# Tying staged weight loads to the first attention's last copy to x

## The chip, the cores and the metric

One NeuronCore of a Trainium2 chip runs the whole program. The metric is device time in microseconds (us) of one execution. Medians are over single runs; all runs of this case were of the fast state. Where two kernels are compared, the ratio is the mean time of one kernel's fast runs over that of the other's of the same rounds, so it is not quite the ratio of the medians quoted beside it. Its 95% interval follows in brackets.

## The reference, cut to what matters

```python
# attention: (batch, heads, seq, dim) = (4, 8, 768, 48), a gated linear recurrence
f = 1.0 / (1.0 + np.exp(-f_logit))
for t in range(S):
    state = f[:, :, t, :, None] * state + np.einsum('bhd,bhe->bhde', k[:, :, t], v[:, :, t])
    y[:, :, t] = np.einsum('bhd,bhde->bhe', q[:, :, t], state)
x = y.transpose(0, 2, 1, 3).reshape(B, S, H * D)          # (4, 768, 384)
# mixer, per batch
u  = x + (x.transpose(0, 2, 1) @ U @ V).transpose(0, 2, 1)
ch = np.maximum(u @ w_ch1, 0.0) @ w_ch2                   # 384 -> 1536 -> 384
return u + ch
```

The weights arrive as 64-bit floating-point numbers and are turned into 32-bit ones on the chip. The attention inputs are 32-bit already.

## The kernel before

Four batches, each of four pairs of heads (16 "units"). The attention of batch 0 runs first, alone; its mixer runs while the attention of batch 1 goes on, and so forth. The change touches the seam between the attention of batch 0 and its mixer. There, weights come in by loads of 384 KB, called pieces here: w1 pieces 0 to 11, of 128 columns each. `start` issues a load; `end` converts it, with two instructions on ACT (lines L90, L91), three on DVE and one on GpSimd.

```python
def start():                                  # weight_loader
    raw = pool.tile([P, WP], U64, name="w_raw", bufs=RAW) if place is None else place()
    raw = T["raw"] = raw[0:rows, 0:n]
    dma.dma_start(out=shaped(raw), in_=w)
def end():
    ...
    nc.scalar.activation(f, hi.bitcast(F32), AF.Abs)                 # L90
    nc.scalar.activation(r, lo, AF.Copy, scale=2.0**-29)             # L91
    nc.vector.tensor_scalar(...)              # three on DVE
    nc.gpsimd.tensor_tensor(...)
# ahead_by(n, loads): call i starts load i + n and ends load i
```

The first six w1 pieces are staged in the "zw" buffers, which nobody needs yet, two pieces to a buffer; all others share four "w_raw" buffers.

```python
FIRST = 6                                     # early = 3: U and two parts of V
weights += [take_in(w1[:, :, i * P : (i + 1) * P], w1_rows[...], place if i < FIRST else None) for i in range(NFC)]
...
for n in range(HP):                           # the attention of batch 0, units 0 to 3
    ...
    if n == 1:
        for start, _ in weights[: early + 2]: # U, V, V, w1 pieces 0 and 1
            start()
    elif n > 1:
        load(n + 2, "f", "k", "q", "v")       # inputs of units 4 and 5
for start, _ in weights[early + 2 : early + FIRST]:   # w1 pieces 2 to 5
    start()
loads = ahead_by(early + FIRST, weights)
for piece in rear(HP - 1, "read") + loads[:2] + rear(HP - 1, "inner") + loads[2 : early + 1]:
    piece()                                   # "inner" of unit 3 ends with the last copy to x
loads = loads[early + 1 :]
m = mixer(0)
start = m.before[:5] + m.firsts[0:1] + m.before[5:]
idles = {1: 1, 2: 1}
for i, (_, piece) in enumerate(start + m.firsts[1:]):
    busy(idles.get(i, 0))                     # idle matmuls
    piece()
    if loads and i != 1:
        loads.pop(0)()                        # one conversion (and one more start) a step
    ...
```

The steps of `start` are: 0 the low-rank product (ph), 1 its sum (ph), 2 the mixing (pu, and the additions to x on DVE), 3 and 4 two turns of x (put on TensorE, copy uT on ACT), 5 the first product with w1 (pz), 6 the third turn. In the traces TensorE, DVE and ACT run these steps in the order of the program (ACT in the kernel before: h at 52.05 us, piece 2 at 52.76 and 53.22, uT at 55.55). The order in which SyncE issues transfers is fixed when the program is built, from the program's order and a model of what is ready when; the trace of the kernel before has it so, from q of unit 5 at 47.08 over pieces 2 and 3 at 47.96, v at 50.73 and pieces 4 and 5 at 52.82 to pieces 6 and 7 from 54.46 on.

Of the kernel before, what the change touches and what calls it, by code (L numbers as in the profile page):

```python
# [10 lines left out]
F32 = mybir.dt.float32  # L11
U32 = mybir.dt.uint32
U64 = mybir.dt.uint64
# [5 lines left out]
WP = 384  # L19
# [82 lines left out]
def ahead_by(n, loads):  # L102


    def call(i):
        if i + n < len(loads):
            loads[i + n][0]()
        loads[i][1]()

    return [lambda i=i: call(i) for i in range(len(loads))]  # L110
# [322 lines left out]
def factored_path(ctx, tc, q, k, v, f_logit, moe_U, moe_V, moe_w_ch1, moe_w_ch2, out, ok):  # L433
# [4 lines left out]
    nc = tc.nc  # L438
    B, H, S, D = q.shape
    P = nc.NUM_PARTITIONS  # L440
# [4 lines left out]
    HP = H // 2  # L445
# [4 lines left out]
    NFC = FF // P  # L450
# [17 lines left out]
    zp = ctx.enter_context(tc.tile_pool(name="zp", bufs=3))  # L468
# [21 lines left out]
    def load(n, *names):  # L490

        b, hp = divmod(n, HP)
        for nm in names:
            if nm == "v":
                v_tiles[n] = three.tile([P, NBL, 2, D], F32, name="v_nat")
            for par in range(2):
                head = src[nm][b, 2 * hp + par]
                if nm == "v" and par:

                    for s in range(2):  # L500
                        nc.sync.dma_start(
                            out=v_tiles[n][(1 - s) * C : (2 - s) * C, :, par, :],
                            in_=head.rearrange("(c s p) d -> s p c d", s=2, p=C)[s],
                        )
                    continue
                if nm == "v" or n < TURNED:
                    dst = v_tiles[n] if nm == "v" else nat[n % 2][nm]
                    nc.sync.dma_start(out=dst[:, :, par, 0:D], in_=head.rearrange("(c p) d -> p c d", p=P))
                    continue
                head = head.rearrange("(c i) d -> i c d", i=NB)  # L510
                for part in range(2):
                    p0 = par * PAD + part * NB
                    n_ch = min(NB, D - part * NB)
                    nc.sync.dma_start(
                        out=raw[n % 2][nm][p0 : p0 + NB, :].rearrange("p (c d) -> p c d", d=NB)[:, :, 0:n_ch],
                        in_=head[:, :, part * NB : part * NB + n_ch],
                    )
# [43 lines left out]
    table = one.tile([P, 1], F32, name="table")  # L561
# [7 lines left out]
    weights = [take_in(U, moe_U.rearrange("(c p) r -> p c r", p=P))]  # L569
    weights += [take_in(*pair) for pair in by_rows(V, moe_V, R)]  # L570
    early = len(weights)
    w1_rows = moe_w_ch1.rearrange("(c p) f -> p c f", p=P)

    spare = []

    def place():
        if not spare:
            t = zp.tile([P, NFC // 2, 2 * P], F32, name="zw").rearrange("p i t -> p (i t)").bitcast(U64)
            spare.extend([t[:, 0:WP], t[:, WP : 2 * WP]])
        return spare.pop(0)  # L580

    FIRST = 6
    weights += [
        take_in(w1[:, :, i * P : (i + 1) * P], w1_rows[:, :, i * P : (i + 1) * P], place if i < FIRST else None)
        for i in range(NFC)
# [96 lines left out]
    def mixer(b):  # L682
        return Mixer(tc, b, x_tiles[b], U, V, w1, w2, sums if b else None, ident, blocks, out, two, three, zp, ps_big, ps_mm,
                     b == 0, z_all, room if b >= B - 2 else None, FEWER - (b - B + 2) * NCH // 4)
# [172 lines left out]
    def front(n, *names):  # L857

        if n >= NU:
            return []  # L860
        if n not in ahead:
            ahead[n] = dict(zip(("gates", "keep", "keys", "read_back", "queries"), prepare(n)))
        return [ahead[n].pop(nm) for nm in names]

    def rear(n, *names):

        if not 0 <= n < NU:
            return []
        if n not in here:
            here[n] = dict(zip(("kept", "states", "scan", "scores", "read", "inner"), attend(n)))  # L870
        return [here[n].pop(nm) for nm in names if nm in here[n]]

    def steps(first, last):


        for n in range(first, last):
            yield from rear(n - 1, "scores") + rear(n, "kept") + front(n + 1, "gates", "keep", "keys")
            yield from rear(n - 1, "read")
            made = rear(n, "states", "scan")
            yield lambda: [f() for f in made]  # L880
            yield from front(n + 1, "read_back", "queries") + rear(n - 1, "inner")
            if n + 2 < NU:
                load(n + 2, "v")

    def attention(pieces, portions, todo):

        fill = Fill(todo, portions)
        for piece in pieces:
            fill()
            piece()  # L890
        fill.rest()
# [10 lines left out]
    def start_mixer(b, after):  # L902

        m = mixer(b)
        n = len(after) // 4
        pieces = after[:n] + m.before[:1] + after[n : 2 * n] + m.before[1:2] + after[2 * n : 3 * n]
        pieces += m.before[2:3] + after[3 * n :] + m.before[3:]
        for _, piece in pieces:
            piece()
        return m  # L910
# [4 lines left out]
    with tc.manual_schedule(engines={nc.vector.engine, nc.scalar.engine}):  # L915


        idle = ps_mm.tile([P, 512], F32, name="idle", tag="mm")

        def busy(n):  # L920
            for _ in range(n):
                nc.tensor.matmul(idle[:, 0:DM], lhsT=ident, rhs=ends[:, 0:DM], start=True, stop=True)  # L922

        busy(1)
        for piece in front(0, "gates"):
            piece()
        for n in range(HP):
            pieces = front(n, "keep", "keys") + rear(n - 1, "scan", "scores")
            pieces += [lambda: busy(3)] + rear(n, "kept") + front(n, "read_back", "queries")
            if n + 1 < HP:  # L930
                pieces += front(n + 1, "gates") + rear(n - 1, "read", "inner") + rear(n, "states")
            else:
                pieces += rear(n, "states") + rear(n - 1, "read") + rear(n, "scan", "scores") + rear(n - 1, "inner")
            for piece in pieces:
                piece()
            if n < 2:
                load(n + 2, "v")
            if n == 1:


                for start, _ in weights[: early + 2]:
                    start()
            elif n > 1:
                load(n + 2, "f", "k", "q", "v")
        for start, _ in weights[early + 2 : early + FIRST]:
            start()
        loads = ahead_by(early + FIRST, weights)
        for piece in rear(HP - 1, "read") + loads[:2] + rear(HP - 1, "inner") + loads[2 : early + 1]:
            piece()
        loads = loads[early + 1 :]  # L950

# [4 lines that stand above are left out]
        EARLY = 9  # L956
        second = chain(front(HP, "gates", "keep", "keys", "read_back", "queries"), steps(HP, 2 * HP + 1))
        for i, (_, piece) in enumerate(start + m.firsts[1:]):
            busy(idles.get(i, 0))
            piece()  # L960
            if loads and i != 1:
                loads.pop(0)()
            if i >= EARLY:
                next(second)()
        for f in loads:
            f()
        n = len(m.seconds) // (NBL // 2)
        todo, after = m.seconds[:-n], m.seconds[-n:]

        attention(second, 12 + 10 * HP - (len(start) + len(m.firsts) - 1 - EARLY), todo)  # L970
        m = start_mixer(1, after)
        for f in to_sum:
            f()
# [325 lines left out]
@with_exitstack  # L1299
def kernel(  # L1300
    ctx: ExitStack,
    tc: tile.TileContext,
    q: bass.AP,
    k: bass.AP,
    v: bass.AP,
    f_logit: bass.AP,
    moe_U: bass.AP,
    moe_V: bass.AP,
    moe_w_ch1: bass.AP,
    moe_w_ch2: bass.AP,  # L1310
    out: bass.AP,
):


    nc = tc.nc
    args = (q, k, v, f_logit, moe_U, moe_V, moe_w_ch1, moe_w_ch2, out)
    flag = ctx.enter_context(tc.tile_pool(name="flag", bufs=1))
    ok = flag.tile([1, 1], I32, name="ok")
    with ExitStack() as inner:
        factored_path(inner, tc, *args, ok)  # L1320
    good = nc.values_load(ok[0:1, 0:1], min_val=0, max_val=1)
    with tc.If(good == 0):
        with ExitStack() as inner:
            general_path(inner, tc, *args)
# [30 lines left out]
```

## Time and profile before

| | before |
|---|---|
| median of the first three runs (range) | 492.71 us (492.5 to 496.79) |
| span of the profiled run | 490.9 us |
| TensorE (PE) busy | 472.4 us, 96% |
| DVE, ACT, GpSimd busy | 73%, 33%, 7% |

The head of the profile's page of the kernel before (busy us, share of the span, instructions):

```profile
span 490.9 us, 12677 instructions
...
PE 472.4 (96%) x5519; PEld 402.0 (82%) x5519; DVE 356.1 (73%) x561; ACT 163.4 (33%) x307; POOL 36.3 (7%) x49
```

TensorE's timeline at the seam (start, duration, engine, line, operation, out<-in, how many instructions; in brackets the idle time before and what ended it):

```profile
52.67 1.56 PE L197 MATMUL pu<-h,V 32*128 32x384 f32 x12
54.64 1.74 PE L207 MATMUL put<-ident,x 128*128 128x128 f32 x12 [0.40 <-DVE x L187]
56.49 2.83 PE L219 MATMUL pz<-uT,w 128*128 128x256 f32 x12
59.16 0.82 PE L207 MATMUL put<-ident,x 128*128 128x128 f32 x6
```

PE is the engine to look at, the others have room. It goes from pu over the turns into pz with one gap of 0.40 us. From there on it is full (busy for all of the 55.5 us from 56.5 to 112), so the seam is where time can be won or lost. The four lines of the timeline are the ones to compare later.

### The profile page before, as it was taken

To read this page: it belongs to the slowest core of one execution; us is meant where nothing else is said; L and a number is where in the kernel's file an instruction comes from. 1 tells how busy PE (TensorE), PEld (TensorE's weight loads), DVE (VectorE), ACT (ScalarE), POOL (GpSimd) and SP (SyncE) were. 2 spreads that over 40 slices of the span, in tenths; PEclk is the share of its full clock that TensorE was granted. 3 is DMA by queue.
4 is the path that set the end of the run, shared out by engine and by line. 5 is a ranking of instruction groups with operands and counts; after the bars stand their busy time and mean duration, and the time that the engine had idled before them with its cause. 6 is when DMAs were issued, how large, how long until landed. Compare 5 with 4: busy or idle time off the path is not lost.

```text
span 490.9 us, 12677 instructions
## 1 busy us (share of the span) xinstructions
PE 472.4 (96%) x5519; PEld 402.0 (82%) x5519; DVE 356.1 (73%) x561; ACT 163.4 (33%) x307; POOL 36.3 (7%) x49
## 2 busy tenths in 40 slices
PE   7997999999999999999999999999989999999995
PEld 4775688886666568898898788889969999999995
DVE  5886789788998667656855449796876796948642
ACT  3434675564443223423242322442311212112200
POOL 3001345451000000000000000000000000000000
PEclk9999999999999999999999999999989999999998
DMA  9989976685768422424534100100000000000001
GB/s 144 158 172 172 260 183 147 158 153 65 113 106 123 83 41 37 62 27 91 65 49 81 25 33 1 27 3 19 18 2 0 34 2 16 17 1 33 0 34 38
DMA packets 158679, 34.34 MB, mean 70 GB/s; under 512 B 149206, under 2 KB 157078, under 8 KB 158614
## 3 DMA queue, kind: packets, MB, share of 16 engines
q1 hardware_dynamic: 158614, 33.44, 37.3%
q8 instruction: 45, 0.74, 0.7%
q14 instruction: 20, 0.16, 0.1%
HBM read 28.70 MB, written 4.72 MB: 68 GB/s over the span
## 4 chain that ended last, share of the span: by engine, by line
PE 90%; DVE 4%; DMA 2%; issue 1%; ACT 1%; SPq 0%; DVEq 0%; ACTq 0%
PE pw L273 25%; PE pz L219 23%; PE pp L371 12%; PE po L244 10%; PE y L823 3%; PE y L841 3%; PE ds L785 3%; PE sc L748 3%; PE pt L620 2%; PE idle L922 2%; PE put L207 2%; PE pt L769 2%; DMA late<-in_f_logit_dram 1%; PE pu L197 1%; DMA late<-in_k_dram 1%
## 5 line engine op out<-in xcount | busy, mean ns | idle before, releaser
L219 PE MATMUL pz<-uT,w 128*128 128x256 f32 x504 | 115.8, 384 | 0.1
L219 PEld LDWEIGHTS pz<-uT,w 128*128 128x128 f32 x504 | 93.4, 190 | 13.2 <-issue 0.3
L273 PE MATMUL pw<-zw,w_raw 128*128 128x192 f32 x216 | 37.4, 328 | 0.8 <-DVE o L187 0.8
L273 PE MATMUL pw<-w,z_all 128*128 128x192 f32 x216 | 37.8, 330 | 0.2 <-DVE o L187 0.2
L273 PEld LDWEIGHTS pw<-zw,w_raw 128*128 128x128 f32 x216 | 35.2, 190 | 1.6 <-DVE o L187 1.5
L273 PEld LDWEIGHTS pw<-w,z_all 128*128 128x128 f32 x216 | 34.9, 190 | 1.2 <-DVE o L187 0.8
L654 DVE TENSOR_TENSOR_SCAN late<-fz,late 128x768 f32<-128x768 f32 x16 | 28.1, 1755 | 9.7 <-ACT fz L649 5.1
L95 POOL TENSOR_TENSOR w<-w_y,w_r 128x384 int32<-128x384 int32 x24 | 30.2, 1257 | 36.2 <-DVE w_y L94 32.1
L229 ACT ACTIVATE z_all<-pz 128x512 f32<-128x512 f32 x33 | 19.6, 595 | 39.6 <-PE pz L219 39.5
L371 PE MATMUL pp<-v_nat,late 128*128 128x128 f32 x224 | 28.8, 275 | 0.0
L672 DVE TENSOR_TENSOR_SCAN late<-fz,other 128x768 f32<-128x768 f32 x16 | 27.9, 1745 | 0.1
L371 PEld LDWEIGHTS pp<-v_nat,late 128*128 128x128 f32 x224 | 27.0, 192 | 0.0
L244 PE MATMUL po<-w,zw 128*128 128x384 f32 x72 | 25.6, 499 | 0.0
L244 PE MATMUL po<-w,z_all 128*128 128x384 f32 x72 | 25.3, 496 | 0.0
L364 ACT ACTIVATE other<-other 128x512 f32<-128x512 f32 x18 | 11.3, 631 | 40.0 <-DVE other L187 40.0
L811 ACT COPY st<-added 128x576 f32<-128x576 f32 x12 | 14.7, 1226 | 26.0 <-DVE added L806 26.0
L755 DVE TENSOR_TENSOR A<-sc,causal 128x768 f32<-128x768 f32 x16 | 15.2, 947 | 10.5 <-PE sc L748 10.5
L244 PEld LDWEIGHTS po<-w,zw 128*128 128x128 f32 x72 | 12.9, 190 | 8.7 <-issue 1.2
L244 PEld LDWEIGHTS po<-w,z_all 128*128 128x128 f32 x72 | 13.1, 190 | 8.5 <-DVE o L187 0.6
L92 DVE TENSOR_SCALAR w_y<-w_y 128x384 f32<-128x384 f32 (+3 forms) x27 | 11.9, 439 | 10.9 <-ACT w_y L90 10.7
L187 DVE TENSOR_TENSOR w_raw<-z_all 128x768 f32<-128x768 f32 x12 | 11.4, 954 | 10.6 <-ACT z_all L229 9.2
L187 DVE TENSOR_TENSOR w_y<-w_y,pw 128x192 f32<-128x192 f32 x18 | 6.3, 349 | 17.5 <-PE pw L273 17.5
(185 smaller groups left out, 844.7 us busy)
## 6 DMA issues: line engine op xcount, KB each, us to landing
w_raw<-in_moe_w_ch_dram SPq DMA_DIRECT2D x18, 384.0 KB, 4.3
out_dram<-o SPq DMA_DIRECT2D x24, 192.0 KB, 1.9
v_nat<-in_v_dram SPq DMA_DIRECT2D x16, 144.0 KB, 2.8
v_nat<-in_v_dram SPq DMA_DIRECT2D x32, 72.0 KB, 3.0
zw<-in_moe_w_ch_dram SPq DMA_DIRECT2D x6, 384.0 KB, 5.5
late<-in_f_logit_dram SPq DMA_DIRECT2D x10, 96.0 KB, 3.4
late<-in_k_dram SPq DMA_DIRECT2D x10, 96.0 KB, 2.8
late<-in_q_dram SPq DMA_DIRECT2D x10, 96.0 KB, 2.9
```

The source lines that it names most:

```text
L95: nc.gpsimd.tensor_tensor(dst.bitcast(I32), shaped(y.bitcast(I32)), shaped(r), ALU.add)
L187: nc.vector.tensor_tensor(*args)
L219: nc.tensor.matmul(pm[:, i * 2 * P : (i + 1) * 2 * P], lhsT=w1[:, m, o : o + P], rhs=uT[a][:, m, :], start=(m == 0), stop=(m == NDC - 1))
L229: nc.scalar.activation(z[a, c][:, k : k + 2, :].rearrange("p i t -> p (i t)"), pm, AF.Relu)
L244: nc.tensor.matmul(pm, lhsT=z[a, i // NI][:, i % NI, s * P : (s + 1) * P], rhs=w2[:, i, :], start=(i == 0), stop=(i == NFC - 1))
L273: nc.tensor.matmul(pm[:, n * HM : (n + 1) * HM], lhsT=lhs[:, i, :], rhs=rhs[:, i, :], start=(i == 0), stop=(i == NI - 1))
L371: nc.tensor.matmul(pm[:, i, r * P : (r + 1) * P], lhsT=room["w"](wn)[:, r * P : (r + 1) * P], rhs=x_node(a, xn), start=((xn, wn) == of[0]) ...
L654: nc.vector.tensor_tensor_scan(backwards(X, S - 1, S), backwards(f, S, S), backwards(ends, S - 1, S), 0.0, ALU.mult, ALU.add,)
L672: nc.vector.tensor_tensor_scan(Y, f[:, 0:S], starts, 0.0, ALU.mult, ALU.add)
L748: nc.tensor.matmul(sc[part[s ^ par], par, c * C : (c + 1) * C], lhsT=T["k"][rows[par], chunk[2 * c + s]], rhs=T["q"][rows[par], chunk[2 * ...
L755: nc.vector.tensor_tensor(T["A"], sc[:, :, 0 : NBL * C].rearrange("p h (c i) -> p h c i", i=C), causal.unsqueeze(1).unsqueeze(1).broadcast ...
L785: nc.tensor.matmul(ds[par * PAD : (par + 1) * PAD, s, c * D : (c + 1) * D], lhsT=T["kb"][part[s ^ par], par, i, :], rhs=vt[part[s ^ par], ...
```

## The change

Its intent: the loads of w1 pieces 2 to 5 should not compete for the DMA engines with what the first attention still reads. To tie them to its end, all three zw buffers are taken at the start, GpSimd writes one column of the second one, and ACT reads this column right after the last copy to x. The load of piece 2 overwrites the column, so it must wait for that read. The loads of pieces 6 and 7 (in `loads[:2]`) now stand ahead of pieces 2 to 5 in the program.

```diff
--- before.py
+++ after.py
@@ -573,13 +573,17 @@
 
     spare = []
 
+    FIRST = 6
+    for _ in range(FIRST // 2):
+        t = zp.tile([P, NFC // 2, 2 * P], F32, name="zw").rearrange("p i t -> p (i t)")
+        spare.extend([t[:, 0 : 2 * WP], t[:, 2 * WP : 4 * WP]])
+
+    held = spare[2][:, 0:1]
+    nc.gpsimd.memset(held, 0.0)
+
     def place():
-        if not spare:
-            t = zp.tile([P, NFC // 2, 2 * P], F32, name="zw").rearrange("p i t -> p (i t)").bitcast(U64)
-            spare.extend([t[:, 0:WP], t[:, WP : 2 * WP]])
-        return spare.pop(0)
-
-    FIRST = 6
+        return spare.pop(0).bitcast(U64)
+
     weights += [
         take_in(w1[:, :, i * P : (i + 1) * P], w1_rows[:, :, i * P : (i + 1) * P], place if i < FIRST else None)
         for i in range(NFC)
@@ -942,10 +946,13 @@
                     start()
             elif n > 1:
                 load(n + 2, "f", "k", "q", "v")
+        loads = ahead_by(early + FIRST, weights)
+        for piece in rear(HP - 1, "read") + loads[:2] + rear(HP - 1, "inner"):
+            piece()
+        nc.scalar.copy(table, held)
         for start, _ in weights[early + 2 : early + FIRST]:
             start()
-        loads = ahead_by(early + FIRST, weights)
-        for piece in rear(HP - 1, "read") + loads[:2] + rear(HP - 1, "inner") + loads[2 : early + 1]:
+        for piece in loads[2 : early + 1]:
             piece()
         loads = loads[early + 1 :]
 
```

## The prediction

> **What bounds the kernel now.** I read four views, from the whole to the place of the change. First the page: TensorE is busy 472.4 of 490.9 us, so what matters is where it still waits. The chain that ended last, read from the end of the first attention (batch 0) on:
>
> ```profile
> 44.21 1.43 issue
> 45.64 0.95 PE y L841 x47
> 46.59 0.02 issue
> 46.61 0.65 ACT x L847
> 47.26 0.14 issue
> 47.40 2.27 PE ph L172 x12
> ...
> 53.62 0.97 DVE x L187
> 54.59 0.04 issue
> 54.64 1.74 PE put L207 x12
> 56.37 0.12 issue
> 56.49 2.83 PE pz L219 x12
> ```
>
> The copy to x that the change names is "ACT x L847": it ends at 47.26. After it come the low-rank product, two turns of x (put) and, at 56.49, the first product with the big weights (pz). From 56.49 to 112 the stretches show TensorE busy for the whole time, so **any delay of that first pz is a delay of the end**, and nothing between here and 47 waits for a transfer: the bound is TensorE and the ACT and DVE steps that feed it.
>
> Second, the queue that issues transfers (SyncE), from the end of attention's loads on:
>
> ```profile
> 47.08 0.84 SPq L508 DMA_DIRECT2D other<-in_q_dram  x1
> 47.96 2.68 SPq L81 DMA_DIRECT2D zw<-in_moe_w_ch_dram  x2
> 50.73 0.44 SPq L508 DMA_DIRECT2D v_nat<-in_v_dram  x1
> 51.23 1.55 SPq L501 DMA_DIRECT2D v_nat<-in_v_dram  x2
> 52.82 1.60 SPq L81 DMA_DIRECT2D zw<-in_moe_w_ch_dram  x2
> 54.46 0.49 SPq L81 DMA_DIRECT2D w_raw<-in_moe_w_ch_dram  x1
> ```
>
> The zw lines are the four loads concerned: w1 pieces 2 and 3 at 47.96 and 49.8, pieces 4 and 5 at 52.82 and 53.5. **They already start after 47.26**, held back only by their place in the queue. The v between them is v of unit 5, needed far later.
>
> Third, ACT, which converts the weights in between its other work:
>
> ```profile
> 52.05 0.48 ACT L182 COPY h<-ph 128x384 f32<-128x384 f32 x1 [0.97 <-PE ph L180]
> 52.76 0.56 ACT L90 ACTIVATE w_y<-zw 128x384 f32<-128x384 f32 x1 [0.23 <-DMA zw<-in_moe_w_ch_dram]
> 53.22 0.54 ACT L91 ACTIVATE w_r<-zw 128x384 int32<-128x384 uint32 x1
> 55.55 0.80 ACT L208 COPY uT<-put 128x768 f32<-128x768 f32 x1 [1.79 <-PE put L207]
> 56.25 0.55 ACT L90 ACTIVATE w_y<-zw 128x384 f32<-128x384 f32 x1
> ```
>
> Piece 2 lands at about 52.7 and ACT takes it at once, having waited 0.23 us for it. The next instruction of ACT is the copy uT that pz at 56.49 reads. That copy is ready to go at 55.55, and the two conversions take 1.0 us (52.76 to 53.76), so **piece 2 may land at most until about 54.55**: 1.8 us of slack.
>
> Fourth, the stretches, for transfers and the clock:
>
> ```profile
> 44.54:47.95 3.41, 1.47 (x55) 1.11 (x56) 2.09 (x7) 1.64 (x6) 1.04 (x2) 1.00 0.97 168
> 47.95:51.37 3.42, 3.42 (x11) 1.41 (x6) 2.31 (x7) 2.01 (x5) 1.45 (x2) 0.50 1.02 148
> 51.37:54.78 3.41, 2.99 (x17) 1.32 (x17) 1.79 (x4) 1.48 (x3) 1.00 (x1) 1.00 1.06 278
> 54.78:58.19 3.41, 3.29 (x20) 2.67 (x20) 3.31 (x7) 2.39 (x4) 0.48 (x1) 1.00 0.99 259
> 58.19:61.60 3.41, 3.41 (x21) 3.03 (x20) 3.31 (x6) 2.42 (x6) 1.51 (x2) 1.00 1.04 332
> ```
>
> The last three columns are granted clock, DMA share and GB/s. The DMA engines are full (0.97 to 1.06) through all of it: what is put ahead of piece 2 makes it later. And a stretch in which TensorE was busy 1.47 of 3.41 us is followed by one at half clock.
>
> [...]
>
> **The change, part by part.**
> - Added: a one-column memset on GpSimd in the prologue (off the path), and on ACT a copy of one column after the copy to x. The alike copy "seen" (128x2) takes 0.16 to 0.17 us. It delays the conversion of the last piece of V, which has some microseconds before pu at 52.67. Cost 0 to 0.1 us.
> - The wait itself: it is fulfilled at about 47.26 + 0.2 = 47.5, before the queue was free for these loads (47.96). Direct cost 0.
> - **Moved: the order of issue.** The loads of pieces 6 and 7 (calls loads[:2]) stand ahead of pieces 2 to 5 in the program now. Piece 6 needs no wait (a fourth w_raw buffer is free; before, it is issued at 54.46 without one), piece 7 only the conversion of U (over at 45.1). SyncE issues in order, and its order is fixed at build time from readiness, so I expect: q of unit 5, piece 6, v of unit 5, piece 7, pieces 2, 3, 4, 5, then 8 and 9.
>
> When does piece 2 land? A weight piece is 384 KB = 0.393 MB, v of unit 5 is 288 KB = 0.295 MB. Bytes moved from 47.95, by the stretches: 0.51 MB by 51.37, 1.45 by 54.78, 2.34 by 58.19. Some 0.45 MB of the start belongs to k and q of unit 5, issued before (an estimate: with it pieces 2 and 3 would be done at 0.45 + 0.79 = 1.24 MB; piece 3 landed 5.1 us after 49.8, at 54.9, which fits roughly). In the new order piece 2 is done at 0.45 + 0.393 + 0.295 + 0.393 + 0.393 = 1.92 MB: 54.78 + (1.92 - 1.45) / 0.259 = 56.6. As transfers interleave, it may be 58 (the w_raw load at 54.46 took 6.8 us to land). I take 57.2.
>
> Then ACT converts at 57.3 to 58.3, copies uT until 59.1, and pz starts at 59.2 instead of 56.49: **+2.7 us**. The other conversions have room: pieces 2 and 3 are needed by the 13th pz group of the second column pair at about 65 (before, GpSimd finished them at 58.7 and 60.7), and that point shifts too.
>
> TensorE would then idle from 56.45 to 59.2. [...]before, 1.94 us idle in a window (3.41 - 1.47) brought half clock. Half clock for 3.41 us of work costs 1.7 us. I give it 0.6: **+1.0 us**. Sum: 492.7 + 2.7 + 1.0 = 496.4.
>
> **Rivals.**
> 1. *No change of order that matters*: piece 7 isn't ahead, so piece 2 is done at 1.53 MB, about 55.1, 0.6 us past the slack. Then 493 to 493.5. For it: the order is settled by modelled times that I don't see. Against: v and piece 6 are ready earlier by the program's order in any case.
> 2. *Piece 8 goes ahead too* (its wait, V's conversion, ends at about the time of the copy to x): piece 2 at 2.32 MB, 58.1, or 59 with interleaving; pz +3.6 to +4.5, half clock likely: 498 to 499.5.
> 3. *The intent works*: [...]the 1.43 us stall and the half clock after it (another 1.2 us or so in ph, 2.27 us for 12) vanish: 490. Against: these loads start 2.3 us after that stall's end.
> 4. *DVE becomes the bound* when conversions bunch up: DVE is busy 21.53 of 23.5 us from 56.5 to 80. But it is shifted together with TensorE, so I add nothing.
>
> **Range and chances.** Main line 55%, 495 to 498; rival 1 20%; rival 2 15%; rival 3 7%. This gives 496.3 us, 8 in 10 between 492.4 and 500. Two per cent is 9.9 us: none of these lines reaches 502.6, so within 2% gets 0.95.
>
> **What would show it.** In the changed kernel's SyncE queue, w_raw loads stand before the zw loads and the first of these zw loads is issued at about 52.5. On ACT the conversion L90 of piece 2 waits 4 to 5 us for DMA zw; uT and the first pz come 2 to 4 us late; a half-clock stretch follows at about 58 to 62. The 1.43 us of issue at 44 stays. It would be wrong if the zw loads still stand first after q, if ACT no longer has piece 2 ahead of uT, or if TensorE's wait before pz shows up no longer at the end because a later wait was absorbed.

## The result, and the profile after

| | before | after |
|---|---|---|
| median (range), 6 runs each | 493.07 us (492.5 to 496.79) | 499.08 us (498.03 to 500.57) |
| ratio of fast runs | | 1.0108 [1.0072, 1.0144] |
| span of the profiled run | 490.9 us | 497.7 us |
| PE busy | 472.4 us | 474.0 us |

The change costs 1.1%: the interval excludes no change, and it lies within the 2% of "same". The span grew by 6.8 us; TensorE's busy time grew by only 1.6 of them, so most of it is waiting. The head of its page:

```profile
span 497.7 us, 12677 instructions
...
PE 474.0 (95%) x5519; PEld 403.4 (81%) x5519; DVE 356.3 (72%) x561; ACT 163.0 (33%) x308; POOL 36.4 (7%) x50
```

The work is the same but for one instruction on ACT and one on GpSimd. TensorE's timeline at the seam of the changed kernel:

```profile
53.05 1.56 PE L197 MATMUL pu<-h,V 32*128 32x384 f32 x12
55.01 1.74 PE L207 MATMUL put<-ident,x 128*128 128x128 f32 x12 [0.40 <-DVE x L187]
61.20 4.51 PE L219 MATMUL pz<-uT,w 128*128 128x256 f32 x12 [4.45 <-ACT uT L208]
65.55 0.82 PE L207 MATMUL put<-ident,x 128*128 128x128 f32 x6
```

Two things are new: 4.45 us of waiting for ACT's copy uT ahead of pz, and pz itself takes 4.51 us in place of 2.83. The issue queue (SyncE) shows why the first came about:

```profile
47.01 0.70 SPq L508 DMA_DIRECT2D other<-in_q_dram  x1
47.76 1.93 SPq L81 DMA_DIRECT2D w_raw<-in_moe_w_ch_dram  x1
49.73 1.04 SPq L81 DMA_DIRECT2D zw<-in_moe_w_ch_dram  x1
50.86 0.43 SPq L508 DMA_DIRECT2D v_nat<-in_v_dram  x1
51.35 1.45 SPq L501 DMA_DIRECT2D v_nat<-in_v_dram  x2
52.92 0.54 SPq L81 DMA_DIRECT2D w_raw<-in_moe_w_ch_dram  x1
53.98 1.57 SPq L81 DMA_DIRECT2D zw<-in_moe_w_ch_dram  x3
```

The built program tells which piece each line is. Of the four zw loads only one carries a wait for ACT, that of piece 2, because only it overwrites the held column. (That of piece 7 waits for ACT too, but for the conversion of U, as it did before.) The order is: piece 6, **piece 3**, v of unit 5, piece 7, **piece 2** (with the wait), 4, 5. Before, it was 2, 3, v, 4, 5, 6, 7. So piece 2 went from the first place to the fifth, and its issue from 47.96 to 53.98. ACT's timeline then:

```profile
52.43 0.48 ACT L182 COPY h<-ph 128x384 f32<-128x384 f32 x1 [0.44 <-PE ph L180]
59.39 0.54 ACT L90 ACTIVATE w_y<-zw 128x384 f32<-128x384 f32 x1 [6.48 <-DMA zw<-in_moe_w_ch_dram]
59.84 0.54 ACT L91 ACTIVATE w_r<-zw 128x384 int32<-128x384 uint32 x1
60.28 0.78 ACT L208 COPY uT<-put 128x768 f32<-128x768 f32 x1
```

ACT stands 6.48 us in front of piece 2. The copy uT behind it had its input from about 55.9 on (the first six of the twelve put instructions, as before) and comes at 60.28. The second new thing shows in stretches that are cut where the granted clock changes in this trace (at 61.44 and 64.85, 3.41 us apart), and as far apart ahead of that (length, then for each engine busy time and count in the order PE, PEld, DVE, ACT, POOL; the last three columns are granted clock, DMA share and GB/s):

```profile
54.61:58.02 3.41, 1.74 (x12) 1.27 (x12) 2.08 (x3) 0.00 (x0) 0.00 (x0) 1.00 1.03 226
58.02:61.44 3.42, 0.24 (x1) 0.27 (x2) 1.28 (x3) 2.05 (x5) 0.00 (x0) 1.00 1.09 355
61.44:64.85 3.41, 3.41 (x9) 2.72 (x9) 3.21 (x5) 2.09 (x5) 2.00 (x2) 0.50 0.87 207
```

A stretch in which TensorE was busy for 0.24 of 3.42 us is followed by one at half clock (0.50), just when pz begins. The DMA engines are full (1.03, 1.09) while piece 2 is under way.

**Where the 6.8 us went**, by the starts of single instructions in the two traces: 0.38 us before the first pu (a longer wait for which the profile shows no releaser, "issue", 1.73 against 1.43 us, and other small differences of the run); 4.33 us from the first pu to the first pz (8.15 against 3.82); 1.69 us from there to the thirteenth pz instruction (5.01 against 3.32: the half clock); -0.14 us up to the 37th. From the 37th pz at 71.39 to the instruction of the same number far behind, at 292.91, the shift stays at 6.26 us. About 0.5 us more is picked up after that in waits that differ from run to run.

### The profile page after: what moved, and what is told of

Same layout as the page of the kernel before. It is cut to its first block, busy times and chain, and to the rows that moved or that the text cites. A ratio compares the mean times of both kernels' runs of the same rounds, so it can differ in the third digit from the quotient of the medians.

```text
span 497.7 us, 12677 instructions
## 1 busy us (share of the span) xinstructions
PE 474.0 (95%) x5519; PEld 403.4 (81%) x5519; DVE 356.3 (72%) x561; ACT 163.0 (33%) x308; POOL 36.4 (7%) x50
## 4 chain that ended last, share of the span: by engine, by line
PE 88%; DVE 4%; DMA 3%; issue 2%; ACT 1%; SPq 1%; DVEq 0%; ACTq 0%
PE pw L273 24%; PE pz L219 23%; PE pp L371 12%; PE po L244 10%; PE y L827 3%; PE y L845 3%; PE ds L789 3%; PE sc L752 3%; PE pt L624 2%; PE idle L926 2%; PE pt L773 2%; PE put L207 1%; DMA late<-in_f_logit_dram 1%; DMA zw<-in_moe_w_ch_dram 1%; PE ph L172 1%
## 5 line engine op out<-in xcount | busy, mean ns | idle before, releaser
L219 PE MATMUL pz<-uT,w 128*128 128x256 f32 x504 | 117.4, 388 | 4.5 <-ACT uT L208 4.5
L219 PEld LDWEIGHTS pz<-uT,w 128*128 128x128 f32 x504 | 94.8, 193 | 17.7 <-issue 4.7
L92 DVE TENSOR_SCALAR w_y<-w_y 128x384 f32<-128x384 f32 (+3 forms) x27 | 14.8, 548 | 17.6 <-ACT w_y L90 17.3
L759 DVE TENSOR_TENSOR A<-sc,causal 128x768 f32<-128x768 f32 x16 | 15.2, 948 | 10.2 <-PE sc L752 10.2
L845 PEld LDWEIGHTS y<-v_nat,A 64*64 64x64 f32 x768 | 13.0, 134 | 7.4 <-issue 5.6
```

Source lines behind the costliest of these rows:

```text
L219: nc.tensor.matmul(pm[:, i * 2 * P : (i + 1) * 2 * P], lhsT=w1[:, m, o : o + P], rhs=uT[a][:, m, :], start=(m == 0), stop=(m == NDC - 1))
L759: nc.vector.tensor_tensor(T["A"], sc[:, :, 0 : NBL * C].rearrange("p h (c i) -> p h c i", i=C), causal.unsqueeze(1).unsqueeze(1).broadcast ...
L845: nc.tensor.matmul(o(s, par, c), lhsT=T["A"][part[s ^ par], par, c, :], rhs=vt[part[s ^ par], c, par, :], start=False, stop=True, skip_gro ...
```

## The experiments

**My theory**: the time of the seam is set by when piece 2 lands, because ACT takes it, in the program's order, before the copy uT that pz needs. The wait, the copy on ACT and the memset cost next to nothing themselves. **Rivals**: A, it is pieces 6 and 7 going ahead, whichever piece waits; B, the wait or the copy on ACT holds things up as such; C, contention or the later loads of w2 make the time; D, the half clock costs nothing.

For every run I read three times off the trace, all counted from the first pu, since its own start varies by 1.9 us from trace to trace (52.28 to 54.21), with the "issue" wait at 44 us and with one or two stretches of half clock behind it (47.95 to 51.37 in the kernel before, 46.00 to 52.82 with the wait on piece 4, 6 and 7 behind): when ACT takes piece 2, when the first pz starts, and when the 37th pz instruction starts (fourth group of twelve; by then all effects of the seam are over).

| run | order of the loads (w = waits for ACT's read of the held column) | ACT takes piece 2 | first pz | 37th pz | half clock at first pz | median, us | ratio to before |
|---|---|---|---|---|---|---|---|
| before | 2 3 v 4 5 6 7 | 0.09 | 3.82 | 12.46 | no | 493.07 | |
| after | 6 3 v 7 2w 4 5 | 6.34 | 8.15 | 18.34 | yes | 499.08 | 1.0108 [1.0072, 1.0144] |
| after again | 6 3 v 7 2w 4 5 | 4.84 | 6.66 | 15.16 | no | 497.95 | 1.0107 [1.0075, 1.0140] |
| order only | 6 2 v 7 3 4 5 | 2.75 | 4.58 | 14.64 | no | 494.70 | 1.0030 [1.0006, 1.0054] |
| wait on piece 4 | 6 2 v 7 3 4w 5 | 2.71 | 4.56 | 14.38 | no | 494.40 | 1.0029 [1.0002, 1.0056] |
| wait, 6 and 7 behind | 3 4 v 2w 5 6 7 | 5.91 | 7.73 | 17.92 | yes | 497.88 | 1.0082 [1.0059, 1.0105] |
| wait on piece 4, 6 and 7 behind | 2 3 v 4w 5 6 7 | -0.25 | 3.81 | 12.45 | no | 494.13 | 1.0004 [0.9976, 1.0032] |
| copy on ACT only | 2 3 v 4 5 6 7 | 0.80 | 3.82 | 12.46 | no | 494.07 | 1.0014 [0.9992, 1.0037] |
| after, converting later | 6 3 v 7 2w 4 5 | 5.94 | 3.82 | 13.49 | no | 496.94 | 1.0076 [1.0053, 1.0099] |
| before, converting later | 2 3 v 4 5 6 7 | 3.59 | 3.83 | 12.33 | no | 496.19 | 1.0051 [1.0015, 1.0088] |
| after, 13 idle matmuls | 6 3 v 7 2w 4 5 | 6.75 | 11.93 | 20.36 | no | 499.78 | 1.0136 [1.0101, 1.0172] |
| after, 6 idle matmuls | 6 3 v 7 2w 4 5 | 7.29 | 9.10 | 17.61 | no | 496.27 | 1.0058 [1.0034, 1.0083] |
| before, two more idle matmuls | 2 3 v 4 5 6 7 | -0.03 | 3.82 | 12.47 | no | 493.94 | 1.0015 [0.9988, 1.0042] |

One rule covers the columns in all rows where the conversion stands ahead of uT and no idle matmuls overrun: **first pz = the later of 3.82 and "piece 2 taken" + 1.82**. After: 6.34 + 1.81 = 8.15. Order only: 2.75 + 1.83. Wait, 6 and 7 behind: 5.91 + 1.82. The 1.82 us are the two conversions, the copy uT and the step to TensorE (after: 0.45, 0.44, 0.78 and 0.14 us).

How late piece 2 comes is not only a matter of its place: the five traces with the queue of the changed kernel have it at 4.84 to 7.29. Much of this is when SyncE gets to the first weight load at all (47.3 to 50.2 us). Counted from that issue, ACT takes piece 2 after 4.0 to 4.8 us with nothing ahead (in the three traces of that queue in which ACT waited for it), 5.3 and 5.9 with piece 6 ahead, 9.0 with two pieces and v ahead, and 10.2 to 11.6 with three pieces and v. So what stands ahead does set how late it is. From issue to landing alone, piece 2 took 4.7 us before (issued at 47.96) and 5.3 us after (issued at 53.98).

### The new order without the wait

```diff
-    held = spare[2][:, 0:1]
-    nc.gpsimd.memset(held, 0.0)
...
-        nc.scalar.copy(table, held)
```

> The change without its wait: the memset and the one-column copy on ACT are gone, the new program order stays. The built queue has the same shape as the changed kernel's, piece 6, one zw piece, v of unit 5, piece 7, three zw pieces; only that the piece in the early place is 2 and not 3. My theory (the time is set by when piece 2 lands, because ACT takes it before the copy uT that pz needs): piece 2 lands at about 55, the first pz starts at about 57, no half clock at 61; piece 3 now lands late (59.3) and stands before the second uT, which costs some 0.8 us more. 494.0 to 495.0 us. Rival A (the pieces 6 and 7 put ahead are the cost, whichever piece waits): as slow as the changed kernel, 498 to 500.

Measured: 494.70 us, ratio 1.0030. Pieces 6 and 7 are as far ahead as in the changed kernel; 2 and 3 have swapped places. ACT's timeline of this run:

```profile
55.03 0.57 ACT L90 ACTIVATE w_y<-zw 128x384 f32<-128x384 f32 x1 [2.89 <-DMA zw<-in_moe_w_ch_dram]
...
55.94 0.78 ACT L208 COPY uT<-put 128x768 f32<-128x768 f32 x1
59.35 0.56 ACT L90 ACTIVATE w_y<-zw 128x384 f32<-128x384 f32 x1 [2.64 <-DMA zw<-in_moe_w_ch_dram]
```

Piece 2 lands at 55.0, and the late one is now piece 3, at 59.35 (in the changed kernel the load in this place was piece 2, at 59.39). It stands behind the first uT and in front of the second. No half clock followed TensorE's three short waits (0.88, 0.76 and 0.26 us): twelve pz took 2.83 and 2.86 us. Rival A falls: the same bytes ahead cost 0.30% here (some 1.5 us) and 1.08% there (5.3 us).

### The wait on another piece

```diff
-    held = spare[2][:, 0:1]
+    held = spare[4][:, 0:1]
```

> The changed kernel with one number changed: the column that is held lies in piece 4 and not in piece 2. Same memset, same copy on ACT, same shape of queue, with piece 2 in the early place (piece 6, 2, v, 7, 3, 4 with the wait, 5). My theory: as without the wait at all, 494.0 to 495.0. Rival B (the wait on ACT's copy as such holds the queue up): as slow as the changed kernel, 498 to 500.

Measured: 494.40 us, 1.0029. One index in the changed kernel takes away more than two thirds of its cost. The wait is still there, on a load that nobody is in a hurry for. ACT's timeline has piece 2 in the early place:

```profile
55.97 0.57 ACT L90 ACTIVATE w_y<-zw 128x384 f32<-128x384 f32 x1 [2.85 <-DMA zw<-in_moe_w_ch_dram]
```

Rival B falls for the wait.

### The wait without pieces 6 and 7 ahead

```diff
-        for piece in rear(HP - 1, "read") + loads[:2] + rear(HP - 1, "inner"):
+        for piece in rear(HP - 1, "read") + [weights[0][1], weights[1][1]] + rear(HP - 1, "inner"):
...
-        for start, _ in weights[early + 2 : early + FIRST]:
+        for start, _ in weights[early + 2 : early + FIRST + 2]:
```

> The wait without the pieces 6 and 7 ahead: their loads start behind those of pieces 2 to 5. The built queue is piece 3, piece 4, v of unit 5, piece 2 (with the wait on ACT), piece 5, pieces 6 to 9. My theory: piece 2 has lost its place to 3 and 4 and to v, lands at about 57.8, TensorE waits some 3 us before the first pz, and a half clock follows: 496.5 to 498. Rival A (pieces 6 and 7 ahead are the cost): 492.5 to 493.5.

Measured: 497.88 us, 1.0082, as expected. With 6 and 7 out of the way, the pieces 3 and 4, which do not wait for anything, step into the first two places, v follows, and piece 2 is issued fourth. ACT's line at the seam, and TensorE's (its wait of 4.03 us is longer than the 3 that I expected):

```profile
58.56 0.54 ACT L90 ACTIVATE w_y<-zw 128x384 f32<-128x384 f32 x1 [6.06 <-DMA zw<-in_moe_w_ch_dram]
```

```profile
60.38 4.51 PE L219 MATMUL pz<-uT,w 128*128 128x256 f32 x12 [4.03 <-ACT uT L208]
```

One piece fewer is ahead than in the changed kernel. From the first pu, piece 2 is 0.43 us earlier (5.91 against 6.34), which is less than the spread between traces; from the first weight load's issue it is 9.0 us against 10.2 to 11.6. The half clock follows as well. So the loads of 6 and 7 are not the cause by themselves: the held load loses its place at the head of the queue to whatever is not held.

### The wait on piece 4, pieces 6 and 7 behind

The two edits above together.

> The wait kept whole (memset, copy on ACT, a load waiting for it), but on piece 4 in place of 2, and pieces 6 and 7 behind: the built queue is that of the kernel before, 2, 3, v, 4 (with the wait), 5, 6 to 9. My theory: as fast as before, 492.5 to 494, with 12.3 to 12.7 us from the first pu to the fourth group of twelve pz. Rival B (the wait as such, the copy or the memset cost something): 495 or more.

Measured: 494.13 us, ratio 1.0004 [0.9976, 1.0032]; 12.45 us from the first pu to the 37th pz, as before. TensorE's timeline:

```profile
53.87 1.56 PE L197 MATMUL pu<-h,V 32*128 32x384 f32 x12
55.83 1.74 PE L207 MATMUL put<-ident,x 128*128 128x128 f32 x12 [0.40 <-DVE x L187]
57.68 2.83 PE L219 MATMUL pz<-uT,w 128*128 128x256 f32 x12
```

Memset, copy and wait are all there and cost nothing that can be seen. The median lies 1.1 us over the one beside it (493.01) and just above my range, the means do not differ; the seam in the trace decides. The first pu is late here (53.87), but that is not the copy: TensorE starts the low-rank product 0.14 us after the copy to x, as before, and then has two stretches of half clock (46.00 to 52.82, granted clock 0.50) in place of one (47.95 to 51.37). Between this kernel and the one of the section above, only the index of the held column differs: 1.0004 with the wait on piece 4, 1.0082 on piece 2. Here the wait was free where it didn't change the order of what is needed soon.

### The copy on ACT only

```diff
-... + rear(HP - 1, "inner") + loads[2 : early + 1]:
+... + rear(HP - 1, "inner") + [lambda: nc.scalar.copy(table, ident[:, 0:1])] + loads[2 : early + 1]:
```

> The kernel before with the one-column copy on ACT alone, reading a constant, behind the copy to x; no load waits for it and the queue is that of before. My theory: it lies beside TensorE's wait for x and costs 0 to 0.2 us: 492.5 to 493.5. Rival B (the copy on ACT delays the first attention's end and all behind it): 494 or more.

Measured: 494.07 us, 1.0014 [0.9992, 1.0037]. By its number this median is where I put rival B (494 or more), but the kernel before gave 493.37 beside it, and the interval holds 1. The seam in the trace is that of before to 0.01 us (3.82 and 12.46), and the wait of TensorE for the copy to x stays 0.84 us. The copy took 0.20 us. The times alone would leave up to 0.4% open; the trace shows no place where the copy could cost it.

### ACT's order

```diff
-            if loads and i != 1:
+            if loads and i not in (1, 2):
```

in the changed kernel, so that every conversion from piece 2 on stands one step later and the first uT goes ahead of piece 2.

> The changed kernel, its queue unchanged up to the ninth piece, but every conversion from piece 2 on stands one step later in ACT's order, so that the first uT no longer stands behind piece 2. My theory (ACT's order turns a late load into a wait of TensorE): the first pz starts at about 57 although piece 2 still lands at about 59.3; the second uT, now behind piece 2, costs about 0.8 us; no half clock. 494 to 495.5. Rival C (DMA contention or the later loads of w2 make the time): 498 to 500, with a wait elsewhere.

Measured: 496.94 us, 1.0076: more than expected. The seam did as the theory says. ACT's timeline:

```profile
56.19 0.80 ACT L208 COPY uT<-put 128x768 f32<-128x768 f32 x1 [3.02 <-PE put L207]
59.25 0.55 ACT L90 ACTIVATE w_y<-zw 128x384 f32<-128x384 f32 x1 [2.26 <-DMA zw<-in_moe_w_ch_dram]
```

Piece 2 is as late as ever (5.94 us after the first pu), but pz starts at 3.82 as before, no half clock follows, and the 37th pz comes at 13.49. **So it is ACT's order that turns the late load into TensorE's wait**, and the seam's cost falls from 5.9 to 1.0 us with an unchanged queue. The time, however, fell by less than that, and the trace had a new wait at 133. Rival C remained possible for that part, so I ran the same edit on the kernel before:

> The kernel before with only the later conversions of the earlier run (from piece 2 on one step later in ACT's order). That run with the changed kernel took 3.6 us over before where I expected 1 to 2. In its trace 1.0 us was lost before the fourth group of pz and another 1.1 us at about 133, where TensorE waited 0.63 us in the second attention. If the later conversions themselves cost that second part, this one is 1 to 2 us over before, 494 to 495.5, with the same wait near 131. If not, 492.5 to 493.5.

Measured: 496.19 us, 1.0051 [1.0015, 1.0088]. TensorE's timeline of the two runs, before with later conversions first:

```profile
133.85 0.92 PE L841 MATMUL y<-v_nat,A 64*64 64x48 f32 x48 [0.63 <-ACT seen L830]
```

```profile
134.10 0.92 PE L845 MATMUL y<-v_nat,A 64*64 64x48 f32 x48 [0.63 <-ACT seen L834]
```

The same wait in both, with no held load in the first of them. From the 37th pz to the 101st instruction of the later products (pw) the two runs need 222.86 and 222.85 us, the kernel before 221.52. So in the traces 1.3 us of the experiment on the changed kernel belongs to the edit itself and 1.0 us to the seam. The times hold more than that: both runs missed their ranges on the high side, the edit alone costs 0.51% (about 2.5 us) and with the changed queue 0.76% (about 3.7 us), with overlapping intervals. Where the rest lies is open. The edit is a clean test of the seam and no remedy.

### The half clock by itself

Idle matmuls ahead of the first pz, in the changed kernel, to keep TensorE at work without shortening the wait.

```diff
-        idles = {1: 1, 2: 1}
+        idles = {1: 1, 2: 1, 5: 13}
```

> The changed kernel with 13 idle matmuls of 128x384 before the first pz, about 0.33 us each, 4.3 us in sum, to fill TensorE's wait without shortening it. My theory: the first pz starts as late as in the changed kernel (61.2), but no half clock follows at 61.4, so its 12 matmuls take 2.8 us and not 4.5: 1.7 us less than the changed kernel, 497 to 498. Rival D (the half clock costs nothing or comes anyway): 498.5 to 500.

Measured: 499.78 us. This one missed, by my own sizing: one idle matmul is two instructions here and takes 0.65 us, so thirteen took 8.4 us and overran the wait by 4. No half clock followed (the twelve pz took 2.75 us), but pz started at 11.93 us after the first pu. With six, and the changed kernel beside it:

> The filling again, sized rightly: one idle matmul of 128x384 is two instructions and takes 0.65 us, so the thirteen of the earlier run took 8.4 us and overran the wait by 4. Here six, 3.9 us, of the 4.45 us wait. My theory: the first pz starts when piece 2 allows it, 8.1 to 8.3 us after the first pu as in the changed kernel, no half clock follows, and its 12 instructions take 2.8 us and not 4.5: about 1.7 us less than the changed kernel run beside it, 497 to 498 if that gives 499. Rival D (half clock comes anyway or costs nothing): the same time as the changed kernel.

> The changed kernel once more, beside the filled one and the kernel before on one chip, for the ratio between them and as a second trace of the wait: 498 to 500 us, piece 2 taken up by ACT 6 to 7 us late, first pz 8.1 to 8.3 us after the first pu, half clock after it.

Measured: 496.27 us with six idle matmuls (1.0058 [1.0034, 1.0083]), 497.95 us for the changed kernel beside it (1.0107 [1.0075, 1.0140]): 1.7 us apart, as expected; the intervals overlap, so the size is not settled by the times. TensorE's timeline with six:

```profile
56.10 4.04 PE L926 MATMUL idle<-late,ident 128*128 128x384 f32 x12
61.67 2.83 PE L219 MATMUL pz<-uT,w 128*128 128x256 f32 x12 [1.54 <-ACT uT L208]
```

Piece 2 was taken even later than in the changed kernel's first trace (7.29 against 6.34; my 8.1 to 8.3 us for the first pz came out as 9.10), and yet the twelve pz took 2.83 us and not 4.51. The changed kernel's second trace missed what I expected of it (piece 2 at 4.84, first pz at 6.66, the median just under 498) and shows that the half clock does not come every time:

```profile
60.20 2.83 PE L219 MATMUL pz<-uT,w 128*128 128x256 f32 x12 [2.96 <-ACT uT L208]
```

Here the wait was 2.96 us, spread over two stretches (55.28 to 58.70 and 58.70 to 62.11) in which TensorE was busy 1.74 and 1.91 of 3.41 us, and no half clock followed. Over the six runs of each, the mean granted clock was 0.989 with the six idle matmuls and 0.983 without. Rival D, that the half clock costs nothing, falls by the two traces that have it at the first pz (4.51 us in place of 2.83, after waits of 4.45 and 4.03): it is a second cost of the wait, 1.7 us when it comes. That the six idle matmuls are what kept it away is my estimate from the mean clocks; it was not shown, as the half clock also stayed away once without them.

How long TensorE was busy does not settle by itself whether half clock follows. Busy for 0.24 (after, from 58.02), 0.91 (after, from 44.37), 1.19 (before with two more idle matmuls, from 42.72) and 1.47 us (before, from 44.54) of 3.41, it was followed by half clock. At 1.75 (before, from 361.98) it was followed by half clock too, at 1.74 (after, from 54.61, and the trace above, from 55.28) it was not.

### A try for a better kernel

The kernel before has a half clock of its own at 47.95 to 51.37, after TensorE's waits at 44 and 46.6. Two more idle matmuls ahead of the low-rank product were to prevent it.

```diff
-        idles = {1: 1, 2: 1}
+        idles = {0: 2, 1: 1, 2: 1}
```

> The kernel before with two idle matmuls of 128x384 between the first attention and the low-rank product, where TensorE waits 0.84 us for the copy to x. In the window before 47.95 TensorE was idle 1.94 us and half clock followed. If the two take some 0.65 us of that[...], no half clock comes there, ph takes some 1.2 us less and the time is 491.5 to 492.3. If [...]the two matmuls come too late in the window, 492.7 to 493.3.

Measured: 493.94 us, 1.0015 [0.9988, 1.0042]. No gain. Both ranges of the expectation lie below this. In the profiled run the "issue" wait at 44 was 2.00 us and lay in one stretch of 3.41 us (42.72 to 46.13), in which TensorE was busy 1.19 us; half clock came at 46.13 to 49.54 all the same. The two matmuls, 1.3 us at full clock (0.65 each, as above), also outlast the 0.84 us that they were to fill. No version that I ran beats the kernel before.

## Why the prediction was right or wrong

- **The mechanism was right** from the queue on: w_raw loads ahead of zw loads, piece 2 late, ACT standing in front of it, uT and pz late, a half clock after that. Each of these was foretold and is in the trace. The runs with the wait moved to piece 4 and with the later conversions separate the links. What changes the queue was only half seen: the prediction gave it to the new program order, but that order without the wait costs 0.30%, and 1.08% with it. The wait has no direct cost; its indirect cost, a later place for piece 2 in the built queue, is the larger part.
- **"The wait itself: direct cost 0" and "Cost 0 to 0.1 us" for the copy** hold: the run with both, on piece 4 and with the queue of before, has ratio 1.0004.
- **The slack** of piece 2, until 54.55 or 1.9 us after the first pu, was right: the rule above gives 3.82 - 1.82 = 2.0.
- **The step that was mis-sized is the order of issue**, and with it the landing. I expected "piece 6, v of unit 5, piece 7, pieces 2, 3, 4, 5"; the built queue has piece 3 ahead as well. I took all four loads as held, as the change's name says, and did not ask which of them overwrite the held column: only piece 2 does, and 3 had nothing to wait for. With 0.393 MB more ahead, the prediction's own sum gives 2.32 MB and about 58.1, or 59 with interleaving (before, between 53.0 and 53.5 us, 335 packets of under 512 B, nearly all of them v's, and 83 larger ones, the weights', go side by side), which is its rival 2 with another piece in the part of piece 8. Measured: taken at 59.39 in place of 57.3. So +2.7 us for pz became +4.33 from the first pu. The run with two pieces and v ahead of piece 2 has just the bytes that the prediction put there: from the first weight load's issue it took 9.0 us, where the prediction had 57.2 - 47.96 = 9.2. So the sum over bytes was good and the missing piece is what it lacked, though the second trace of the changed kernel (first pz 2.84 us later than before) shows that one trace alone would not settle it. Two of the signs failed with this step: the first zw load went at 49.73 and not at 52.5, and ACT waited 6.48 us and not 4 to 5.
- **The half clock** was put in as 0.6 times 1.7 us = 1.0; in the profiled run it came and took 1.69, in the second trace of the same kernel it did not. Two traces cannot test a weight of 0.6; that the profiled run had it is the luck of that run.
- Both terms together are 6.0 us in the profiled run where the sum had 3.7. The measured 499.08 us lies in the range, 2.8 above the point; it is outside the main line's 495 to 498 and inside rival 2's 498 to 499.5. The chances given add up to 97%, and the mean of the four lines weighted by them is about 495.7 us, not 496.3; that is small beside the miss.
- **Rival 3** (the intent works) fell: the "issue" wait at 44 stayed (1.43 us before, 1.73 after, 1.18 to 2.00 in six other traces), with and without the change, as its loads come after it. What causes that wait was not shown. A 16 KB packet of queue 8, which the page calls "instruction", lands at 44.34 (before) and 44.76 (after), and TensorE goes on 1.30 and 1.29 us after it; no run tests whether the one depends on the other. **Rival 4** (DVE) added nothing that can be seen: the shift is constant at 6.26 us from the 37th pz at 71 to 293.

## What to carry to other kernels

A dependency that is put in to delay a transfer can also change its place in the issue queue (here from the first to the fifth, 47.96 to 53.98 us): ask which loads really carry it, which ones overtake, and which consumer stands first behind the late one in its engine's order (here uT, with its input there from about 55.9 on and run at 60.28). Before delaying a load, work out its slack (last useful landing less present landing; here 1.8 us) and hold the one with most slack: with pieces 6 and 7 behind, the same wait cost 0.82% on piece 2 and nothing that can be seen on piece 4, where the queue stayed as it was. A wait of TensorE can cost more than its length: here 4.45 us of waiting was followed by 3.41 us of half clock that took another 1.69 us, while a wait of 2.96 us was not.
